# One constant of the order: credit per unit of attention between the first layer's products

## The chip, the cores and the metric

The kernel runs on one core of a Trainium2 chip. The metric is the device time of one execution in microseconds, the median of several runs. TensorE (PE) multiplies, VectorE (DVE), ScalarE (ACT) and GpSimd (POOL) do elementwise work, SyncE (SP) issues nearly all DMAs.

## The reference

Three parts follow one another. All inputs are float32 or wider; the output is 1536 x 512 float32.

- Attention: q, k, v of 2 batches x 8 heads x 768 tokens x 64. Each token of q and of k gets a bucket of 6 bits (the signs of its product with `proj`); scores of pairs in different buckets are masked, then softmax, then the product with v. The result is put together to x, 1536 tokens x 512.
- First layer: `h = x @ w_in` (512 x 2048), `g = where(h > 0, h, exp(min(h, 0)) - 1)`, `x = g @ w_out` (2048 x 512).
- Second layer: `h = x @ w_in2`, `g = s * relu(h)**2 + b`, `out = g @ w_out2`.

## The kernel before, in words

**Numbers.** Every float32 operand of a product is split into two float16 parts (high, low), and a product is three matmuls: high x high, low x high, high x low (`products`, L503). The weights come as 64-bit words and are put together on VectorE (L182 to L189) and ScalarE (L176), 512 KB of DMA a piece (`w_load`, L157).

**Attention** is cut into 96 units: one head of one chunk of 128 query tokens. Unit u is chunk u//8, head u%8. A unit is four steps in different engines:
- `u_s` (L330): four matmuls into PSUM (`s`), 128 x 768 scores.
- `u_soft` (L340): VectorE takes the clamped scores and their minimum (L346), ScalarE the exponential with its sum (L348).
- `u_split` (L352): ScalarE makes the high part (`ph`, L367), GpSimd the low part (L370), and SyncE issues a DMA transpose of both (`pt<-ph`, L372).
- `u_av` (L375): 18 matmuls of `pt` with v into `xacc` (L390). It follows `u_s` of the same unit by four or five units.
After the eighth head of a chunk `u_norm` (L401) divides by the sums and a DMA transpose (L414) puts the chunk into x.

The generator `attention()` (L450) writes these: one call (`att_step`, L733) is half a unit. On the way, at units 40 to 48, it also writes the loads and splits of q and k of the second batch.

**First layer.** `moe1` (L549) goes through 6 blocks of 256 tokens (two chunks each). For each block, `up(i)` (L563) writes 16 steps of 12 matmuls 128x256 (tiles `h`), `down(i)` (L584) 16 steps of 12 matmuls (tiles `x2p`). A step's cost is put at 12 * (256/2400 + .003) = 1.316. Each pair of steps of `up` fills one bank of 128x512, which `act1` (L509) empties: ScalarE `e` (L514), VectorE `e` and `g` (L517, L519), ScalarE `gh` (L522), GpSimd `gl` (L525). Steps are numbered `ks`: 0 to 15 `up(0)`, 16 to 31 `down(0)`, 32 to 35 empty ones without cost, 36 to 51 `up(1)`, 52 to 67 `down(1)`, and so on to 195; four empty ones end it. `up(i)` first writes attention until the block's two chunks are done (L565).

**How the two are woven.** After every step the loop at L742 adds its cost to a credit and writes half units of attention as long as the credit holds `sc / 2`:

```
credit += cost
sc = STEP_COST if ks >= SC_N else SC0
while live["att"] and credit >= sc / 2 and may_step():
    credit -= sc / 2
    att_step()
```

`SC0` is 1.2, `SC_N` 16, `STEP_COST` 1.9. Before step 0 the loop at L697 has written 20 units' scores, and 16 units are finished. `may_step` (L446) does not hold anything back with `XB = 6`. When attention is all written, the second layer's first weights are asked for (L750 to L770).

**What the order written is worth.** The program is built under `TileContext(nc, schedule_with_timeline_sim=True)`: the order written is a priority. A scheduler with its own timeline fills each engine's queue, and takes a later instruction ahead of an earlier one that is not ready in that timeline. Each engine's queue is then fixed, and on the chip it is worked through in order.

**Second layer.** `moe2` (L623) comes after all of `moe1`.

Of the kernel before, what the change touches and what calls it, by code (L numbers as in the profile page):

```python
# [47 lines left out]
SPLIT = lambda u: 'act'  # L48
WEV = lambda k: k % 3
W2EV = lambda k: k % 4 == 0  # L50
STEP_COST = 1.9
SC0 = 1.2
SC_N = 16
PRE = 4
# [4 lines left out]
def model_kernel(tc, q, k, v, proj, w_in, w_out, w_in2, w_out2, s2, b2, sel, pop, eye, out):  # L59
# [24 lines left out]
    with ExitStack() as base:  # L84
# [361 lines left out]
        def may_step():  # L446
            u = nxt["av"]
            return u >= NU or blk_of[u // H][0] < in_done[0] + XB
# [234 lines left out]
        if True:  # L683
# [58 lines left out]
            for ks, cost in enumerate(moe1(wi, wo, gp, next_gp, tmp, tmpg, att_step)):  # L742
                if WEV(ks):
                    w1_step()
# [3 lines that stand above are left out]
# [78 lines left out]
```

## Time and profile before

| | us |
|---|---|
| median of 3 runs (747.01 to 753.19) | 752.44 |
| the profiled execution | 750.82 |
| its span in the trace | 748.8 |
| PE busy in the span | 680.8 (91%) |
| DVE, ACT, POOL busy | 473.4, 373.1, 263.1 |

The stages in the trace: to 97 us attention with the loads of the first weights; 97 to 384 us attention and first layer woven together; 384 to 497 us the rest of the first layer alone; from 497 us the second layer. In a table of stretches, "(x...)" is the number of instructions of that engine which touch the stretch, PEld the load of weights into TensorE, PEclk the granted TensorE clock as a share of 2.4 GHz, DMA the mean busy share of the 16 DMA engines.

### The profile page before, as it was taken

To read this page: it belongs to the slowest core of one execution; us is meant where nothing else is said; L and a number is where in the kernel's file an instruction comes from. 1 tells how busy PE (TensorE), PEld (TensorE's weight loads), DVE (VectorE), ACT (ScalarE), POOL (GpSimd) and SP (SyncE) were. 2 spreads that over 40 slices of the span, in tenths; PEclk is the share of its full clock that TensorE was granted. 3 is DMA by queue.
4 is the path that set the end of the run, shared out by engine and by line. 5 is a ranking of instruction groups with operands and counts; after the bars stand their busy time and mean duration, and the time that the engine had idled before them with its cause. 6 is when DMAs were issued, how large, how long until landed. Compare 5 with 4: busy or idle time off the path is not lost.

```text
span 748.8 us, 14405 instructions
## 1 busy us (share of the span) xinstructions
PE 680.8 (91%) x5808; PEld 468.0 (63%) x5808; DVE 473.4 (63%) x890; ACT 373.1 (50%) x632; POOL 263.1 (35%) x199
## 2 busy tenths in 40 slices
PE   2789797888897799989899999999999999999998
PEld 0468576766685577768788888864444444444446
DVE  5799999999776558746568523337988979200000
ACT  2897776752776788867742312225555553010000
POOL 0000356650652458976750311304434452000000
PEclk9999888999999889999999999999999999999999
DMA  9954697896799879998956100001322314010000
GB/s 233 266 170 133 173 236 178 177 216 179 115 234 189 168 108 166 171 176 162 177 96 211 30 2 1 1 29 57 89 80 85 113 57 141 1 56 29 29 28 29
DMA packets 206594, 89.67 MB, mean 120 GB/s; under 512 B 171840, under 2 KB 203072, under 8 KB 206528
## 3 DMA queue, kind: packets, MB, share of 16 engines
q1 hardware_dynamic: 205936, 88.63, 54.0%
q8 instruction: 45, 0.74, 0.4%
q10 hardware_dynamic: 592, 0.14, 0.1%
q14 instruction: 21, 0.17, 0.1%
HBM read 43.13 MB, written 3.15 MB: 62 GB/s over the span
## 4 chain that ended last, share of the span: by engine, by line
PE 53%; DVE 18%; DMA 13%; ACT 8%; issue 5%; POOL 2%; SPq 1%; DVEq 0%; ACTq 0%; POOLq 0%
PE h L506 22%; PE y L506 17%; PE x2p L506 9%; DMA pt<-ph 9%; DVE p L346 4%; DVE e L517 3%; PE s L336 3%; DVE g L519 2%; PE xacc L390 2%; ACT gh L522 2%; DVE wx L183 2%; DMA raw<-in_k 2%; ACT e L514 1%; POOL ph L370 1%; DVE wx L182 1%
## 5 line engine op out<-in xcount | busy, mean ns | idle before, releaser
L370 POOL TENSOR_TENSOR ph<-p,ph 128x768 f16<-128x768 f32 x80 | 134.8, 1697 | 126.4 <-ACT ph L367 109.7
L506 PE MATMUL h<-x,wih 128*128 128x256 f16 x768 | 134.6, 280 | 0.9 <-DVE g L519 0.9
L346 DVE TENSOR_SCALAR_CACHE_REDUCE p<-s 128x768 f32<-128x768 f32 x96 | 90.5, 950 | 30.3 <-PE s L336 26.4
L506 PE MATMUL x2p<-gh,woh 128*128 128x256 f16 x384 | 105.2, 275 | 3.4 <-ACT gh L522 1.1
L506 PE MATMUL h<-x,wil 128*128 128x256 f16 x384 | 107.1, 279 | 0.0
L506 PE MATMUL x2p<-gh,wol 128*128 128x256 f16 x384 | 105.4, 275 | 0.7 <-DVE wol L189 0.7
L506 PE MATMUL x2p<-gl,woh 128*128 128x256 f16 x384 | 105.4, 275 | 0.0
L348 ACT ACTIVATE p<-p,mx 128x768 f32<-128x768 f32 x96 | 89.0, 927 | 32.4 <-DVE mx L347 31.4
L336 PE MATMUL s<-k,q 128*128 128x512 f16 (+1 forms) x384 | 81.0, 340 | 11.5 <-DVE p L346 8.7
L546 POOL TENSOR_TENSOR g2l<-g,g2h 128x512 f16<-128x512 f32 x48 | 57.1, 1194 | 87.2 <-ACT g2h L543 87.2
L506 PE MATMUL h<-x,wi2bh 128*128 128x512 f16 x288 | 85.7, 379 | 0.0
L506 PEld LDWEIGHTS <-wih 128*128 128x128 f16 x768 | 76.6, 100 | 14.2 <-issue 1.8
L525 POOL TENSOR_TENSOR gl<-g,gh 128x512 f16<-128x512 f32 x48 | 56.9, 1186 | 80.0 <-ACT gh L522 80.0
L506 PEld LDWEIGHTS <-woh 128*128 128x128 f16 x768 | 75.1, 98 | 14.0 <-issue 1.7
L390 PE MATMUL xacc<-vv,pt 128*128 128x64 f16 x1440 | 56.5, 197 | 27.0 <-DMA pt<-ph 26.7
L506 PE MATMUL y<-wo2h,g2h 128*128 128x512 f16 (+1 forms) x208 | 75.5, 363 | 0.0
L506 PE MATMUL y<-wo2l,g2h 128*128 128x512 f16 (+1 forms) x208 | 75.5, 363 | 0.0
L506 PE MATMUL y<-wo2h,g2l 128*128 128x512 f16 (+1 forms) x208 | 75.4, 363 | 0.0
L390 PEld LDWEIGHTS <-pt 128*128 128x128 f16 x1440 | 51.7, 100 | 36.9 <-DMA pt<-ph 34.4
L367 ACT ACTIVATE ph<-p 128x768 f16<-128x768 f32 x80 | 65.5, 835 | 7.7 <-DMA pt<-ph 6.2
L506 PEld LDWEIGHTS <-g2h 128*128 128x128 f16 x416 | 40.7, 98 | 42.5
L517 DVE TENSOR_SCALAR e<-e 128x512 f32<-128x512 f32 x48 | 42.7, 891 | 31.8 <-ACT e L514 31.4
(101 smaller groups left out, 1079.6 us busy)
## 6 DMA issues: line engine op xcount, KB each, us to landing
wraw<-in_moe_w_in SPq DMA_DIRECT2D x32, 512.0 KB, 3.7
wraw<-in_moe_w_out SPq DMA_DIRECT2D x32, 512.0 KB, 3.8
raw<-in_k SPq DMA_DIRECT2D x8, 384.0 KB, 4.2
raw<-in_q SPq DMA_DIRECT2D x8, 384.0 KB, 4.2
out<-y SPq DMA_DIRECT2D x11, 256.0 KB, 2.0
v<-in_v SPq DMA_DIRECT2D x4, 384.0 KB, 4.4
raw<-in_v SPq DMA_DIRECT2D x4, 384.0 KB, 4.4
pt<-ph SPq DMA_TRANSPOSE x80, 4.1
```

Of the source, the lines that this page charges most:

```text
L183: nc.vector.scalar_tensor_tensor(out=x, in0=low, scalar=29, in1=x, op0=ALU.logical_shift_right, op1=ALU.bitwise_or)
L336: nc.tensor.matmul(p[:, a0:a1], w[b, hp][:, j, c, :], kf[:, a0:a1], start=(x == 0), stop=(x == 1))
L346: nc.vector.tensor_scalar(f, sps.pop(u), CLAMP, None, op0=ALU.min, op1=ALU.min, accum_out=mx)
L348: nc.scalar.activation(out=f, in_=f, func=ACTF.Exp, scale=-sm / (SQ * SQ), bias=mx, accum_out=sums[b, c][:, h:h + 1])
L367: nc.scalar.activation(out=t[:, 0, :], in_=f, func=ACTF.Copy)
L370: nc.gpsimd.tensor_tensor(out=t[:, 1, :], in0=f, in1=t[:, 0, :], op=ALU.subtract)
L390: nc.tensor.matmul(acc, o[:, C * x + cc, :], vv[:, j, cc, y, :], start=(z == 0 and cc == 0), stop=(z == 2 and cc == C - 1))
L506: nc.tensor.matmul(p, ws[a](kk), xs[b](kk), start=(kk == 0 and z == 0), stop=(kk == n_kk - 1 and z == 2))
L517: nc.vector.tensor_scalar(t["e"], t["e"], SG, SG, op0=ALU.mult, op1=ALU.min)
L519: nc.vector.scalar_tensor_tensor(out=t["g"], in0=t["e"], scalar=-SG, in1=p, op0=ALU.add, op1=ALU.max)
L525: nc.gpsimd.tensor_tensor(out=gl, in0=t["g"], in1=gh, op=ALU.subtract)
L546: nc.gpsimd.tensor_tensor(out=gl, in0=t["g"], in1=gh, op=ALU.subtract)
```

## The change

One constant. From step 16 on, half a unit of attention is written for every 1.25 of credit where it was 0.95. The order before step 16 and every instruction itself are as before.

```
-STEP_COST = 1.9
+STEP_COST = 2.5
```

## Rows read from the trace of the kernel before

**Rows 1.** The page, parts 1 and 2: busy time, and tenths in 40 slices

```profile
PE 680.8 (91%) x5808; PEld 468.0 (63%) x5808; DVE 473.4 (63%) x890; ACT 373.1 (50%) x632; POOL 263.1 (35%) x199
...
PE   2789797888897799989899999999999999999998
```

**Rows 2.** Stretches: from:to, length, PE, PEld, DVE, ACT, POOL busy, PEclk, DMA

```profile
187.00:263.00 76.00, 63.92 (x697) 49.41 (x696) 51.37 (x101) 53.99 (x86) 34.47 (x23) 0.93 0.94 175
263.00:309.00 46.00, 42.52 (x529) 33.82 (x527) 34.13 (x74) 37.13 (x66) 36.86 (x25) 0.96 0.90 146
309.00:318.00 9.00, 9.00 (x114) 7.28 (x113) 6.19 (x18) 8.09 (x16) 7.36 (x6) 1.00 1.06 165
318.00:341.00 23.00, 19.62 (x280) 16.11 (x278) 12.23 (x33) 16.14 (x29) 15.69 (x11) 1.00 1.04 176
341.00:362.00 21.00, 20.01 (x282) 16.46 (x280) 12.42 (x32) 16.29 (x30) 17.55 (x12) 1.00 1.01 172
362.00:384.40 22.40, 20.68 (x300) 18.11 (x301) 13.36 (x26) 13.40 (x25) 14.34 (x11) 1.00 0.89 148
384.40:497.00 112.60, 111.52 (x1019) 99.36 (x1018) 50.84 (x71) 27.67 (x48) 24.32 (x21) 1.00 0.15 46
```

**Rows 3.** Stretches, tile s alone: PE, DVE, PEclk, DMA share, GB/s

```profile
263.00:309.00 46.00, 13.35 (x70) 16.04 (x35) 0.96 0.90 146
309.00:384.40 75.40, 19.41 (x100) 24.60 (x52) 1.00 0.99 165
```

**Rows 4.** Stretches, tile h alone: PE, DVE, ACT, PEclk, DMA share, GB/s

```profile
263.00:309.00 46.00, 24.57 (x189) 4.82 (x7) 4.08 (x7) 0.96 0.90 146
309.00:384.40 75.40, 16.94 (x139) 4.13 (x6) 3.54 (x6) 1.00 0.99 165
```

**Rows 5.** Stretches, tile x2p alone, columns as in the last group

```profile
97.00:187.00 90.00, 23.46 (x192) 0.69 (x1) 0.58 (x1) 0.95 0.89 196
187.00:263.00 76.00, 24.10 (x192) 2.00 (x3) 1.75 (x3) 0.93 0.94 175
...
309.00:384.40 75.40, 23.74 (x192) 1.38 (x2) 1.16 (x2) 1.00 0.99 165
```

**Rows 6.** PE in order of time: start, length, what, idle before

```profile
332.57 0.70 PE L390 MATMUL xacc<-vv,pt 128*128 128x64 f16 x18 [2.68 <-DMA pt<-ph]
333.11 0.81 PE L336 MATMUL s<-k,q 128*128 128x512 f16 x4
333.76 0.27 PE L506 MATMUL x2p<-gl,woh 128*128 128x256 f16 x1
```

**Rows 7.** Lines, 309 to 384.4 us: busy us, mean ns, idle before

```profile
L348 ACT ACTIVATE p<-p,mx 128x768 f32<-128x768 f32 x27 | 25.0, 926 | 12.0 <-DVE mx L347 11.9
...
L367 ACT ACTIVATE ph<-p 128x768 f16<-128x768 f32 x27 | 21.7, 832 | 2.8 <-DMA pt<-ph 2.5
L390 PE MATMUL xacc<-vv,pt 128*128 128x64 f16 x540 | 20.2, 194 | 6.1 <-DMA pt<-ph 6.0
...
L348 ACT ACTIVATION_READ_ACCUMULATOR p<-p,mx 128x1 f32 x27 | 5.0, 187 | 0.0
...
L522 ACT ACTIVATE gh<-g 128x512 f16<-128x512 f32 x6 | 3.8, 625 | 4.8 <-DVE g L519 4.8
...
L514 ACT ACTIVATE e<-h 128x512 f32<-128x512 f32 x6 | 3.5, 590 | 2.2 <-PE h L506 2.2
```

**Rows 8.** The chain that ended last, 384 to 497 us: start, length, what

```profile
390.72 20.96 PE x2p L506 x192
...
423.45 1.00 DVE e L517
...
426.45 1.01 DVE e L517
```

**Rows 9.** SyncE's queue in order of time, after 384 us

```profile
390.91 20.45 SPq L162 DMA_DIRECT2D wraw<-in_moe_w_in  x9
```

## The prediction

> **What bounds the kernel now.** The page comes first: PE is busy 680.8 of 748.8 us, no other engine over 63%, and in the slices PE's 9s are broken only up to the 20th (374 us) and in the last, the kernel's end [rows 1]. So time can come only from PE's holes in the woven stretch. The table of stretches says which: from 187 us on, PE lacks 76.00 - 63.92 = 12.1 us, then 3.5, then 0, 3.4, 1.0 and 1.7 (6.1 from 309 to 384.4), and 1.1 in the 112.6 us of the first layer alone; the second layer, from 497 us, runs none of the woven code. Clock is lost (PEclk under 1.00) before 309 us only [rows 2].
>
> Next, who makes the holes after 309 us: 6.0 of 6.1 us are the `xacc` matmuls waiting for the transposed `pt` [rows 7], while the DMA engines stand at a share of 0.89 to 1.06 [rows 2]. Attention asks for transposes there as fast as they can be had, and PE, in order, stands when one is late [rows 6].
>
> Last, where attention really stands against the order written. Counting matmuls by tile: down(0) and down(1) lie before 263 us, 263 to 309 us holds up(2) (189 of its 192 matmuls show), and after 309 us come all of down(2) and 139 / 12 = 11.6 steps of up(3) [rows 4, 5]. So 309 us is step 84, attention ends after step 111. On the other side 100 / 4 = 25 units' scores lie after 309 us and 70 / 4 = 17.5 in the 46 us before [rows 3]: 71 units have their scores at step 84, 53.5 at step 68.
>
> The order written, by the code: before step 16 credit buys 1.316 / 0.6 half units a step, so 20 + 18 = 38 units stand at step 16, in both kernels. From there a unit costs 1.9 or 2.5 of credit:
>
> - at step 68 (48 costed steps on): 38 + 63.2 / 1.9 = 71 units before, 38 + 63.2 / 2.5 = 63 after; the trace has 53.5.
> - at step 84 (64 on): 38 + 84.2 / 1.9 = 82 before, 38 + 84.2 / 2.5 = 71.7 after; the trace has 71.
>
> So attention was **late against its own priorities** up to the last units. Up to step 84 an instruction of attention went out when its inputs were there, not when credit wrote it, and the wider spread still writes those units earlier than they ran. It begins to bind at step 84, 309 us.
>
> **The change part by part.**
>
> 1. Steps 0 to 15: the same credit, nothing moves: 0.
> 2. Steps 16 to 83, 140 to 309 us: units 38 to 70 are written later, but still ahead of where they ran, so each queue (PE, DVE, ACT, POOL, and SP with the transposes and the second batch's loads) keeps its order. I cost it at 0; what covers it is the lag just counted. Bounds: the holes of 187 to 309 us, 12.1 + 3.5, as a gain, and as a loss another 3.5 [rows 2], the hole of a stretch where both are woven.
> 3. From step 84: units 71 to 95 were woven with 27.6 steps (1.1 a unit); now 2.5 / 1.316 = 1.9 steps a unit, written out at step 137 (the last unit's scores by about 130, then the trailing `u_av`). Some 25 steps of pure product move from behind attention into it. PE's own work: a unit's scores 333.76 - 333.11 = 0.65 us, its `u_av` 333.11 - 332.57 = 0.54 [rows 6], a step 20.96 / 16 = 1.31 [rows 8]. Before: 25 x 0.65 + 540 / 18 = 30 x 0.54 [rows 7] + 27.6 x 1.31 = 68.6 us of work in 75.4, so 6.8 of hole by this count, 6.1 by the table. I take 6.1, the measured one. After: a unit's period is 0.65 + 0.54 + 1.9 x 1.31 = 3.68 us against 75.4 / 25 = 3.02. A transpose every 3.68 us would bring the DMA share from about 1.0 to about 0.82, and `u_av` comes four or five periods (15 us or more) after its scores. The waits for `pt` should go: -6.1.
> 4. What is late next: `up` now has more attention beside it. The nearest row is 263 to 309 us, up(2) with 17.5 units, holes 3.5 us [rows 2]. up(3) gets 16 / 1.9 = 8.4 units, up(4) about 4: in proportion 3.5 x 12.4 / 17.5 = 2.5 us; from below 0, as 309 to 318 us has no hole. I take +1.5, nearer the row with `up` in it.
> 5. Deadlines. up(4) (step 132) needs unit 79, finished about step 108; up(5) (step 164) needs unit 95, finished at 137. Both lead by 24 steps or more, 31 us. The second layer's first weights are asked for once attention is written: 390.91 to 411.4 us on SP's queue [rows 9], now some 28 us later (25 steps at 1.31 less what is won), so to about 440 us, with 50 us in hand before 497. DVE puts them together beside up(4) instead of beside down(3); it is busy 50.84 of 112.6 us there [rows 2]. 0.
>
> **Sum:** -6.1 + 1.5 = -4.6 us. Against its own execution: 750.82 - 4.6 = 746.2. That execution lies 1.6 under the median of the runs, so for a median I say 752.44 - 4.6 = **747.8 us**.
>
> **The measure of PE's idleness, weighed.** By the table PE lacks 6.1 of 75.4 us [rows 2]. The Trainium skill (Perfetto Trace Analysis, Identifying the Most-Contended Engine) holds busy matmul time for a bad measure of the room left, and wants the share of weight loads instead. The sum goes by the table, since the count of work (6.8) nearly agrees with it; the other reading is a rival below.
>
> **The rivals.**
>
> - *ACT's chain holds the banks* (slower). In `up` alone the evictions follow each other at 426.45 - 423.45 = 3.0 us [rows 8], because `gh` waits for `g` before the next `e` can start in ACT's order. A unit adds 926 + 187 + 832 ns = 1.95 us of ACT [rows 7]. Packed, an eviction and its 1.05 units take 0.625 + 0.590 + 2.05 = 3.27 us, under PE's 2 x 1.31 + 1.05 x 1.19 = 3.87; if the units can't fill the gaps of the chain, 3.0 + 2.05 = 5.05, and PE waits 1.18 us an eviction. It decides from 3.87 us of ACT an eviction. Eight evictions in up(3) and about three in up(4): +13.0, less the 6.1: +6.9, 759.3; halved by the four banks in front, +0.4 to +3: 754. Against: at 263 to 309 us ACT was packed to 37.13 of 46 with the same chain [rows 2]. Chance 0.13.
> - *The spread binds from step 16* (it gives more): were attention ahead rather than late, the holes of 187 to 309 us would go too, 15.6 us, and clock of 0.07 x 76 + 0.04 x 46 = 7.2; with the 6.1 and 1.5 left, 725. Against: the two counts at steps 68 and 84. Chance 0.05.
> - *More hidden idleness*: weight loads fill 57.96 of 75.4 us, 77%, and 99.36 of 112.6, 88%, in products alone [rows 2]. At 88% the stretch would take 65.7 us: -9.7, 742.7. Against: score matmuls stream longer for each load, so the share must be lower with attention. The trace's count of work, 68.6 us, speaks against 65.7. Chance 0.10.
> - *It moves nothing that counts*: holes come back at other transposes (queues of the new order are fixed by a timeline which the chip missed by 2.68 us once [rows 6]). -1 to +2: 753. Chance 0.14.
> - My forecast, -3 to -6.8: 745.6 to 749.4: 0.58.
>
> **Numbers.** 1% (7.5 us; the three runs span 6.2) is about what a measurement of this kernel tells from no change. Range 741.5 to 755: the forecast's own, widened by the hidden idleness below, by the ACT chain in its halved form and no gain above, and a run's scatter; it leaves out the full spread and the full ACT chain. Faster by over 1% (under 744.9): hidden idleness and full spread 0.15, and 0.09 of the forecast's low end with scatter: 0.24. Slower by over 1% (over 760): a part of the ACT chain and a bad order: 0.09. Between: 0.67.
>
> **What would show it.** Right: to 309 us the new trace lies on the old one; attention's last `xacc` near 411 instead of 384 us; waits of `xacc` for `pt` after 309 us under 1.5 us in all instead of 6.0; the first layer's end near 492 instead of 497. Wrong in step 2: other holes before 309 us, or 71 units' scores not at step 84. Wrong in step 4: waits of `h` or `x2p` for DVE or ACT in up(3), ACT over 3.87 us an eviction. The whole falls if the second layer's start waits for its weights.

## The result and the profile after

| | before | after |
|---|---|---|
| median of 4 runs, us | 749.92 (747.01 to 753.19) | 742.56 (738.45 to 744.38) |
| profiled execution, us | 750.82 | 743.25 |
| its span, us | 748.8 | 741.1 |

The ratio is 0.9881, 95% interval [0.9848, 0.9915]. Run again it is 0.9898 [0.9873, 0.9923]. The change makes the kernel about 1% faster, 7 to 9 us, where the forecast said 4.6. Its direction held, and its mechanism but for one term; its size did not.

The page of the changed kernel, parts 1 and 2, beside [rows 1]: PE has the same 5808 matmuls, and its last hole of the woven stretch now lies in the 17th slice.

```profile
PE 676.0 (91%) x5808; PEld 466.2 (63%) x5808; DVE 470.6 (63%) x890; ACT 375.5 (51%) x632; POOL 264.2 (36%) x199
...
PE   2689787888897899899999999999999999999998
```

The stretches of the changed kernel (columns of [rows 2]):

```profile
187.00:263.00 76.00, 64.16 (x704) 49.94 (x702) 52.03 (x103) 54.29 (x87) 34.97 (x23) 0.95 0.95 177
263.00:309.00 46.00, 42.16 (x519) 33.33 (x518) 31.82 (x71) 36.82 (x66) 37.09 (x25) 0.93 0.93 150
309.00:337.00 28.00, 28.00 (x337) 23.96 (x334) 13.30 (x31) 16.69 (x28) 16.31 (x12) 1.00 0.73 122
337.00:372.00 35.00, 35.00 (x436) 30.00 (x434) 21.51 (x47) 25.98 (x46) 24.91 (x18) 1.00 0.67 117
372.00:411.90 39.90, 39.90 (x512) 34.87 (x510) 18.98 (x41) 20.31 (x35) 20.00 (x14) 1.00 0.73 117
411.90:497.00 85.10, 84.55 (x752) 72.05 (x750) 44.64 (x69) 24.45 (x44) 20.02 (x17) 1.00 0.22 64
```

Up to 309 us it is the kernel before: holes of 11.8 and 3.8 us where there were 12.1 and 3.5. From 309 us to the end of attention PE is busy 102.9 of 102.9 us; the DMA share, 0.89 to 1.06 before, is 0.67 to 0.73. The lines of that stretch (columns of [rows 7]) show much the same work (100 and 540 matmuls in the kernel before [rows 3, 7]), without a wait for `pt` that was 6.0 us in all:

```profile
L336 PE MATMUL s<-k,q 128*128 128x512 f16 x104 | 21.2, 326 | 0.0
L390 PE MATMUL xacc<-vv,pt 128*128 128x64 f16 x526 | 20.7, 193 | 0.0
```

The size can be read at two marks: the first `x2p` matmul of down(2), which is step 84, and the last start among the `x2p` matmuls of one kind, at the end of down(5). The kernel before, PE in order of time and then the tile x2p (durations, first and last start):

```profile
309.86 0.27 PE L506 MATMUL x2p<-gh,woh 128*128 128x256 f16 x1
```

```profile
L506 PE MATMUL x2p<-gh,woh x384: 269/273/422, 141.6 to 496.5; 128*128 128x256 f16 x192
```

The changed kernel, the same two views:

```profile
309.53 0.27 PE L506 MATMUL x2p<-gh,woh 128*128 128x256 f16 x1
```

```profile
L506 PE MATMUL x2p<-gh,woh x384: 269/273/421, 141.4 to 488.8; 128*128 128x256 f16 x192
```

At step 84 the two stand 0.3 us apart, at the end of the first layer 7.7, and the second layer keeps that distance to its end. So 7.4 us were won between step 84 and step 195. In the repeated run it is 7.2 us (306.79 to 486.2, against 309.86 to 496.5), though its whole span is 10.3 us shorter: 3.1 us of that stood already at step 84, 2.6 of them by the first `x2p` at 139.0 us, where both kernels issue the same order. That is the scatter of one execution.

In the two traces, PE's instructions run in the same order up to 301 us (but for some small matmuls of the bits), DVE's up to 302, ACT's up to 309 and POOL's up to 314; SP issues the same DMAs in the same order from first to last. Unit 71's scores stand at step 86, and the last `xacc` group starts at 411.9 us where the forecast said "near 411".

### The profile page after: what moved, and what is told of

It is laid out like the page before. It is cut to its first block, busy times and chain, and to the rows that moved or that the text cites. A ratio compares the mean times of both kernels' runs of the same rounds, so it can differ in the third digit from the quotient of the medians.

```text
span 741.1 us, 14402 instructions
## 1 busy us (share of the span) xinstructions
PE 676.0 (91%) x5808; PEld 466.2 (63%) x5808; DVE 470.6 (63%) x890; ACT 375.5 (51%) x632; POOL 264.2 (36%) x199
## 4 chain that ended last, share of the span: by engine, by line
PE 61%; DVE 15%; DMA 12%; ACT 6%; issue 4%; SPq 1%; POOL 0%; DVEq 0%; ACTq 0%; POOLq 0%
PE h L506 25%; PE y L506 17%; PE x2p L506 11%; DMA pt<-ph 6%; PE s L336 4%; DVE p L346 3%; PE xacc L390 3%; DVE e L517 2%; DMA q<-src 2%; DVE wx L182 1%; DVE wx L183 1%; DVE g L519 1%; ACT p L348 1%; DMA k<-srcl 1%; DMA raw<-in_k 1%
## 5 line engine op out<-in xcount | busy, mean ns | idle before, releaser
L506 PE MATMUL y<-wo2h,g2h 128*128 128x512 f16 (+1 forms) x208 | 75.4, 363 | 0.0
L506 PE MATMUL y<-wo2l,g2h 128*128 128x512 f16 (+1 forms) x208 | 75.4, 363 | 0.0
L657 ACT ACTIVATE y<-y 128x512 f32<-128x512 f32 (+1 forms) x13 | 7.3, 564 | 97.8 <-PE y L506 96.8
```

The source lines that it names most:

```text
L506: nc.tensor.matmul(p, ws[a](kk), xs[b](kk), start=(kk == 0 and z == 0), stop=(kk == n_kk - 1 and z == 2))
```

## The experiments

The column "behind up(2)" is how much shorter (-) the stretch from the first `h` matmul of up(2), step 68, to the end is than in the kernel before, from one trace each; it leaves out the start's scatter.

| run | ratio to before | 95% interval | behind up(2), us |
|---|---|---|---|
| the change | 0.9881 | 0.9848 to 0.9915 | -6.4 |
| after_again | 0.9898 | 0.9873 to 0.9923 | -7.7 |
| early_only | 0.9963 | 0.9936 to 0.9990 | -1.4 |
| early_dense | 1.0019 | 0.9997 to 1.0041 | +1.6 |
| late_only | 0.9914 | 0.9885 to 0.9943 | -6.5 |
| pace_2_2 | 0.9996 | 0.9973 to 1.0019 | 0.0 |
| slow_end | 0.9907 | 0.9876 to 0.9938 | -8.1 |
| pace_2_8 | 0.9860 | 0.9825 to 0.9895 | -11.5 |
| pace_2_8b | 0.9873 | 0.9837 to 0.9910 | -10.9 |
| pace_3_0 | 0.9924 | 0.9893 to 0.9954 | -5.9 |
| pace_3_2 | 1.0072 | 1.0048 to 1.0096 | +1.0 |
| act_twice | 0.9896 | 0.9863 to 0.9929 | -7.8 |
| half_before | 0.9887 | 0.9818 to 0.9956 | (half transposes) |
| half_after | 0.9807 | 0.9767 to 0.9848 | (half transposes) |
| half_2_2 | 0.9833 | 0.9803 to 0.9863 | (half transposes) |

### The change once more

No edit. 

> The changed kernel once more, to size the gain. Theory A (only units 71 to 95 moved; their holes on PE closed): 7.35 us of the 7.68 by which the two spans differ lie behind step 84, so about -7.3 us, ratio 0.990. Rival B (something before step 84 or in the second layer is faster as well): -9 us or more, ratio under 0.988, and a part of the gain standing before 309 us in the trace.

0.9898, and 7.2 us behind step 84: theory A in size and place. Nothing was won before step 84 or in the second layer that the order explains.

### The part before step 84 alone

```
sc = SC0 if ks < SC_N or ks >= 84 else STEP_COST                       # early_only, STEP_COST 2.5
sc = SC0 if ks < SC_N else STEP_COST if ks < 84 else 0.6               # early_dense, STEP_COST 2.5
```

> Credit of 2.5 a unit from step 16 to 83 only, then 1.2 a unit, so attention is written faster than it can run again. Theory A: the part before step 84 moves nothing, so the holes behind 309 us come back and the time is that of the kernel before: ratio 0.998 to 1.003, waits of xacc for pt after 309 us about 6 us. Rival B (the spread already helps from step 16): at least half of the gain stays, ratio 0.995 or less.

> As early_only, but 0.6 a unit from step 84, so that no product is written between units and attention runs whenever it is ready, as in the kernel before. Theory A: the order of the kernel before, ratio 0.998 to 1.002, xacc waits for pt about 6 us behind 309 us. If the wider spread before step 84 gives something of its own, as early_only's 0.996 lets one think: 0.994 to 0.997, with holes gone before 309 us.

The waits of PE from 309 to 390 us (who for whom: total, times, longest), early_only:

```profile
PE xacc L390 <- DMA pt<-ph: 4.8, 7, 1.2
```

The same view of early_dense:

```profile
PE xacc L390 <- DMA pt<-ph: 6.1, 8, 1.5
```

The waits are back in both. early_dense, in which attention runs whenever it is ready as before, takes the time of the kernel before: the wider spread up to step 83 gives nothing. early_only missed its expectation (0.9963, not 0.998 or more). It still writes a unit evenly every 0.9 step, and its waits are 1.2 us shorter, but the stretch behind step 84 is only 0.1 us shorter. The 2.5 us by which its trace is ahead at step 84 arose while its DVE and ACT still ran the order of the kernel before (to 302 and 308 us). So its trace doesn't explain its 0.4%.

### The part from step 84 alone

```
sc = SC0 if ks < SC_N else STEP_COST if ks < 84 else 2.5               # STEP_COST 1.9
...
credit -= sc / 2
if ks >= 84 or nxt["s"] < 72:
    att_step()
```

> Credit of 1.9 a unit before step 84, held at 72 units' scores, then 2.5 from step 84: only the later part of the change. Theory A: the whole gain, ratio 0.990 (0.987 to 0.993), no waits of xacc for pt over 0.5 us after 309 us. Rival B: half of the gain or less, ratio 0.995 or more.

0.9914, and PE, in the stretches of late_only, lacks 0.5 us from 309 to 384.4 us, none of it for `pt`:

```profile
309.00:384.40 75.40, 74.88 (x925) 64.33 (x924) 40.97 (x93) 49.57 (x86) 49.10 (x34) 1.00 0.77 126
```

Theory A holds: the later half of the change is the change.

### Other paces

```
STEP_COST = 2.2               # 2.8, 3.0 and 3.2 in the other runs
```

> 2.8 a unit. Theory A: the order written meets attention at about step 80 (297 us) instead of 84; the waits of the kernel before between there and 309 us are 0.3 + 1.0 + 0.4 us, so 1 to 2 us more than the change: -8.5 to -9.5 us, ratio 0.988; attention ends near step 151, 13 steps before up(5) needs its last chunk. Rival C (with a lower pace the last chunk comes late, or the second layer's weights do): no better than the change, ratio 0.990 or more, with a wait of h in up(5) or at the start of the second layer.

> The kernel with 2.8 once more, to tell it from the change: 0.986 again (0.984 to 0.989), holes on PE behind 263 us under 2.5 us, against the change's 0.990 and its 3.9 us from 263 to 309 us. If the difference was scatter: 0.989 to 0.991.

Both near 0.987: a lower pace meets attention earlier and closes holes before 309 us too. In the trace of 2.8, as many units have their scores as before up to step 76 (63), and at step 80 it is 65 where it was 67. The stretches of pace_2_8b, beside 3.8 us of hole in the change's 263 to 309 us:

```profile
263.00:309.00 46.00, 44.26 (x548) 37.05 (x546) 30.65 (x69) 36.43 (x63) 38.78 (x27) 1.00 0.80 137
309.00:384.40 75.40, 75.40 (x919) 64.94 (x917) 36.48 (x86) 45.10 (x76) 42.38 (x29) 1.00 0.66 113
```

This is the fastest version with whole transposes, some 0.3% under the change; the intervals overlap, so that alone is not settled. In the traces it is 3 to 5 us ahead behind up(2).

> 3.0 a unit. The order written ends attention at step 161, 3 steps (4 us) before up(5) needs the last chunk, and the norm with its transpose takes about 9 us: a wait of h in up(5) of about 5 us, which takes back half of the gain: ratio 0.990 to 0.996, between 2.8 (0.986) and 3.2 (1.007). If the scheduler can put products of down(4) there: 0.986.

> 3.2 a unit. By the order written the last chunk's units are then not done at step 164, and up(5) forces 2 half units, up(4) 3. If the pace at which the blocks need their chunks bounds the spread: x of the last chunk comes about 9 us (norm, transpose, up to the first h) after its last u_av, PE has no other product to do meanwhile, and the wait of h in up(5), and perhaps in up(4), takes 5 to 10 us: ratio 0.992 to 1.000, worse than 2.8. If the scheduler hides it: as 2.8, 0.986.

Both lose to blocks that wait for their chunks, as expected, 3.0 by 1.9 us in each of two blocks; 3.2 loses more than expected. pace_3_0, waits of PE from 380 to 497 us:

```profile
PE h L506 <- DMA x<-xh: 3.7, 2, 1.9
```

pace_3_2, PE in order of time, the first matmul of up(5):

```profile
457.48 0.58 PE L506 MATMUL h<-x,wih 128*128 128x256 f16 x2 [5.63 <-DMA x<-xh]
```

At 2.8 attention is written out 13 steps before up(5), at 3.0 it is 3, at 3.2 none. Of the 5.0 us by which pace_3_2's span is longer, 3.5 arose already between the first `h` matmuls of up(1) and up(2) (159.6 to 266.8 us, against 159.2 to 262.8), beside waits of the second batch's bits for q. The trace of slow_end (below) shows 3.4 us there at a pace of 2.2, with DVE and ACT in the order of the kernel before, so the pace is not shown to be their cause. But the order of pace_3_2 differs from 161 us on, and all its ten runs lie between 753.3 and 756.5 us, so one run's scatter does not explain it either; why 3.2 lost more than expected stays open.

> 2.2 a unit. Theory A: the order written, 38 + 1.316 / 2.2 units a step from step 20, meets where attention runs at step 91 to 92, about 335 us; of the waits of the kernel before those after that close (1.9 + 0.4 + 0.4 us and small ones, about 3) and the one at the end of up(3) (0.5): -3 to -4 us, ratio 0.995 (0.993 to 0.997). Rival (any wider spread gives the whole gain): 0.990.

This one failed: 0.9996, no gain. Its stretches show the holes closed to 0.7 us up to 384.4 us, and opened behind (a few of the stretches asked for):

```profile
309.00:384.40 75.40, 74.72 (x966) 63.47 (x965) 44.69 (x104) 53.68 (x94) 53.75 (x38) 1.00 0.89 142
384.40:497.00 112.60, 106.96 (x1019) 94.23 (x1018) 45.26 (x74) 27.54 (x48) 25.78 (x21) 0.98 0.24 60
...
390.00:400.00 10.00, 7.43 (x93) 6.14 (x91) 0.40 (x1) 0.12 (x1) 1.24 (x1) 0.83 0.56 80
```

The 5.4 us won come back as 5.6 us of hole behind 384.4 us, where there were 1.1, and with a lower clock on top. 3.6 of the 5.6 lie at attention's tail (2.6 for `pt`, 1.0 for `gl`): after unit 95's scores at 383 us only `u_av` are left, and they follow each other with little between them. Another 0.9 lie in up(4), where `h` waits for DVE, and 1.0 are the waits for `gh` that were there before. PE in order of time at the tail:

```profile
394.33 0.78 PE L390 MATMUL xacc<-vv,pt 128*128 128x64 f16 x18 [2.57 <-DMA pt<-ph]
394.93 0.40 PE L506 MATMUL x2p<-gh,woh 128*128 128x256 f16 x1
395.12 0.42 PE L506 MATMUL x2p<-gl,woh 128*128 128x256 f16 x1
395.33 0.42 PE L506 MATMUL x2p<-gh,wol 128*128 128x256 f16 x1
```

### The tail of 2.2 alone

```
sc = SC0 if ks < SC_N else STEP_COST if ks < 108 else 3.3              # slow_end, STEP_COST 2.2
```

half_2_2 is half_before (below) with STEP_COST 2.2.

> 2.2 a unit to step 107, 3.3 from step 108, so that the last five units and the trailing u_av are spread out beyond down(3) instead of following each other at steps 118 to 123. Theory D (2.2 loses at the tail what it wins before: 5.4 us of holes closed from 309 to 384 us, 2.6 us of wait for a late transpose, 1.0 us for gl, 0.7 us for g and about 1.7 us of clock given back): the tail's waits go, -4 to -6 us, ratio 0.992 to 0.995. Rival E (the pace of 2.2 itself is too dense for the transposes, wherever the tail lies): waits of xacc for pt of 2 us or more remain behind 309 us, ratio 0.997 or more.

> 2.2 a unit with the low part not transposed (its matmuls read the high part). Theory D with a backlog of transposes as the reason of the late one: at half the bytes no wait of xacc for pt over 0.5 us is left at the tail, and the time lies 3 to 5 us under half_before, ratio 0.981 to 0.984. If the tail's order alone is the reason, the wait of about 2 us and its low clock are there still: ratio 0.986 or more.

slow_end has the same pace to step 107 and only its last units spread: 0.9907, better than the 0.992 to 0.995 expected, and behind 384.4 us only 0.7 us of hole is left:

```profile
309.00:384.40 75.40, 73.50 (x949) 62.41 (x947) 45.98 (x104) 51.98 (x90) 54.43 (x37) 1.00 0.89 144
384.40:497.00 112.60, 111.90 (x1107) 98.26 (x1103) 48.43 (x83) 33.40 (x58) 29.44 (x23) 1.00 0.27 65
```

So it was the tail that gave the gain back, not the pace before it. half_2_2 has no wait for `pt` over 0.2 us at the tail, and its ratio of 0.9833 is 0.5% under half_before's. Both fit a backlog, which neither shows itself: at 2.2 the DMA engines are still at 0.89, and transposes that are late by a little would show when `u_av` stop being spread. The wait for `gl` (1.0 us) stayed in half_2_2, so that part is not the transposes'.

### Half of each transpose

These kernels leave out the transposes of the low parts, and the matmuls that read them read the high parts. PE's work stays the same; the output is not the reference's.

```
-nc.sync.dma_start_transpose(out=o, in_=t.rearrange("p x s -> p (x s)"))
+nc.sync.dma_start_transpose(out=o[:, :C], in_=t[:, 0, :])
...
-nc.tensor.matmul(acc, o[:, C * x + cc, :], vv[:, j, cc, y, :],
+nc.tensor.matmul(acc, o[:, cc, :], vv[:, j, cc, y, :],
```

> The kernel before with half of each transpose left out: the low part is not transposed, and its six matmuls read the high part instead, so PE's work is the same. Theory R (rate: the transposes of the woven stretch fill the DMA engines, whose share was 0.89 to 1.06 behind 309 us): the share there falls under 0.8, the waits of xacc for pt behind 309 us fall from 6.0 to under 1.5 us, and the time by 7 us or more. Rival L (latency: one transpose takes its 4 us however much is moved, and the order written puts u_av too near): waits of 3 us or more remain, and the time falls by 3 us or less.

> The changed kernel with the same half of each transpose left out. Theory R: with cheap transposes there is little left for the wider spread to close: within 3 us of half_before. Rival L: the spread gains its 7 us over half_before again.

Neither theory holds alone. half_before's DMA share falls to 0.57 from 309 to 384.4 us, and to 0.60 up to the end of its attention at 370 us, and yet a hole of 2.05 us is left, and 3.2 us of waits for `pt` from 300 us on:

```profile
309.00:384.40 75.40, 73.35 (x958) 62.03 (x957) 48.14 (x105) 51.41 (x87) 52.22 (x36) 0.98 0.57 101
```

```profile
PE xacc L390 <- DMA pt<-ph: 3.2, 2, 2.0
```

A transpose does not take its 4 us however much is moved, as theory L has it. The median from issue to landing in the kernel before, and then in half_before:

```profile
pt<-ph SPq DMA_TRANSPOSE x80, 4.1
```

```profile
pt<-ph SPq DMA_TRANSPOSE x80, 2.8
```

The time falls by 1.1%, but 9.1 us of the 11.1 in its trace stand already at step 84. The spread then gains another 0.8% (half_after), 4.6 us of it behind step 84, against 7.4 with whole transposes. So the traffic of the transposes is a part of what made the holes, and where the order puts `u_av` and the steps around it is another. How much each has can't be read off exactly: with shorter transposes the scheduler writes another order too.

### ACT doubled in up(3)

```
 def hi():
-    nc.scalar.activation(out=gh, in_=t["g"], func=ACTF.Copy)
+    for _ in range(2 if twice else 1):          # twice: block 3 alone
+        nc.scalar.activation(out=gh, in_=t["g"], func=ACTF.Copy)
```

> The changed kernel with gh of up(3) computed twice (the same value), 0.63 us more of ACT an eviction, eight times. If ACT's sum decides (0.63 + 0.59 + 1.05 units of 1.95 = 3.27 us, now 3.90, against PE's 3.87): the same time within 1 us of the changed kernel, ratio 0.990. If the chain e, g, gh decides (3.0 + 0.63 + 2.05 = 5.7 us an eviction): PE waits for banks in up(3), 8 x 1.8 = 14 us, ratio 1.008.

0.9896, the changed kernel's time. up(3) with the doubled `gh`, PE still full, ACT at 28.89 of 35.5:

```profile
336.00:371.50 35.50, 35.50 (x441) 30.44 (x439) 21.32 (x49) 28.89 (x53) 24.47 (x18) 1.00 0.66 118
```

The chain of `e`, `g`, `gh` takes 3.0 us an eviction when alone [rows 8]; if the units could not fill its gaps, PE would have waited, and it did not. So the rival of the held banks is refuted with 0.63 us an eviction to spare.

## Why the prediction was wrong

**Right.** PE's holes as what is to be won; attention late against its own priorities up to step 84, and the spread binding there: late_only has the gain, early_dense none of it, and the queues' orders part at 301 to 314 us. The waits for `pt` gone, the end of attention at 411.9, and the deadlines at 2.5 (2.8 holds them, 3.0 does not). The DMA share fell to 0.67 to 0.73, further than the 0.82 I said. Nine pieces of the second layer's first weights are asked for from 418.4 to 440.6 us, as I said, and nothing waits for them.

**Wrong, step 4** ("what is late next", +1.5 us): it measured 0.0, PE is full to the end of attention. The step that failed is this one: I took the hole of 263 to 309 us as the price of `up` beside attention. Its causes in the kernel before, waits of PE from 263 to 309 us:

```profile
PE xacc L390 <- DMA pt<-ph: 2.5, 4, 1.0
PE s L336 <- DVE p L346: 1.0, 3, 0.4
```

Not one eviction is among them. They are waits of the kind that the spread removes where it binds (at 2.8, which binds earlier, 1.7 us of hole are left in that stretch, at 2.5 still 3.8). So step 4 charged as a new cost what step 3 had just taken away. Asking that stretch who made its hole would have shown it.

**Too small, step 3** (-6.1): two counts differed, and I took the smaller. By work, 68.6 us in 75.4, the hole was 6.8; the table's busy time ends a little late after each group (a 128x256 matmul shows 0.27 us, the next starts after 0.11). And the hole of 1.1 us in 384.4 to 497 us [rows 2] had two halves, one in each of down(4) and down(5), which follow an `up` without attention (x2p waiting for `gh`). Attention now ends inside up(4), and the wait in down(4) is gone: 0.5 us, which I left out. That the one closed the other is argued, not tested. 6.8 + 0.5 = 7.3 agrees with the two marks' 7.4 and 7.2.

That agreement is in part luck: at step 84 the kernel before has the scores of 72 units, not the 71 that I counted, and the changed one of 71. The tile s alone from 309.86 us to the end of the first layer (columns of [rows 3]), before and then changed:

```profile
309.86:497.00 187.14, 18.72 (x96) 23.74 (x52) 1.00 0.49 93
```

```profile
309.86:497.00 187.14, 20.36 (x100) 24.96 (x52) 1.00 0.48 93
```

So the changed kernel has one unit's scores, 0.65 us, more to do behind the mark, and about 8.0 us of holes went. Some 0.7 us of them neither term has.

**The base.** 747.8 us was set against a median of three runs, 752.44. Later rounds of runs put the median of the kernel before at 749.6 to 751.3, and the result at 749.92. Against that last one the forecast said only 0.3%, so even the sum of 4.6 us was lost in part to the scatter of the base.

**The rivals.** Binding from step 16: refuted (early_dense). ACT's chain: refuted (act_twice). Holes that come back at other places: not at 2.5, but this is what 2.2 does at its tail, and the prediction had no sign of how near that was. The hidden idleness, -9.7: 7.4 us were won, which is nearer to the count of work. With PE full and attention woven in, weight loads fill 23.96 + 30.00 + 34.87 = 88.8 of 102.9 us, 86% and not the 88% of products alone. The Trainium skill (Perfetto Trace Analysis, Identifying the Most-Contended Engine) prefers that share, beside the rate of useful operations, to busy time. Here the share pointed to more room, rightly; the 88% that made it 9.7 us, where 7.4 were won, was my choice.

**Open.** Why early_only takes 0.4% less, and why 3.2 loses before up(2); whether the 8.9 us of the first ratio (0.0119 x 749.92) is more than these 7.4 and scatter; and whether 2.8 is faster than 2.5 beyond the runs' noise.

## What to carry to other kernels

Before costing a change of an order written, count in the trace where the work really runs against that order: a knob binds only from the point where the work catches up with it. Then cost the stretch by the work it must hold, and before a hole of a neighbouring stretch is charged as a new cost, ask who made that hole. A pace has two edges besides: the tail, where trailing work loses its cover, and the deadline of the consumer; 2.2 failed at the one, 3.2 at the other.

## What the chip showed that was not expected

A wait of much the same length cost the clock in some places and not in another. After 2.57 us of waiting in pace_2_2 the 128x256 matmuls follow each other every 0.21 us instead of 0.11 (rows at 394.93 and after), the lower level of 1.2 GHz, and the stretch 390 to 400 us has a granted clock of 0.83; after the 2.68 us at 332.57 us of the kernel before [rows 6] the clock stays at 1.00 [rows 2]. Shorter waits cost it too: after 1.97 us of waiting, which end at 340.52 us, half_before has 0.85 from 342 to 352 us with PE full:

```profile
342.00:352.00 10.00, 10.00 (x104) 8.11 (x102) 3.36 (x9) 4.87 (x9) 5.03 (x4) 0.85 0.37 70
```
